# Converting float64 weights to float32 on the chip: 1024 columns at a step, on VectorE and ScalarE alone

## The chip, the cores and the metric

One core of one Trainium2 chip runs the whole program. The metric is the device time of one execution in microseconds (us). Before the change the median of three runs is 1245.48 us (1245.4 to 1246.98). The engines are TensorE (PE, its weight loads PEld), VectorE (DVE), ScalarE (ACT), GpSimd (POOL) and SyncE (SP), which issues most DMAs. Each works through its own queue in order.

## The reference

```python
xread = softmax(scale * x @ state.T) @ state            # attention, per batch and head
sread = softmax(scale * state @ x.T) @ x
x = concat([xread, sread], axis=2) -> (4352 tokens, 512)
x = (x @ w_a) * (x @ w_b) @ w_out                       # w_a, w_b: 512 x 1536, w_out: 1536 x 512
# then a top-1 mixture of 8 experts on the result:
out[mask] = gate * sigmoid * (relu(x[mask] @ w1[e]) @ w2[e])
```

The three weights `w_a`, `w_b` and `w_out` arrive as float64 (the inputs scale them with a float64 factor). TensorE has no float64, so the kernel reads them as pairs of 32-bit words (low word, high word) and builds float32 numbers from the bits.

## The kernel before, in words

Phase 1 computes attention and the first mixture matrix products for eight batches, one after the other (`main(0)` to `main(7)`), and a last part for the state rows (`main_sr`). Phase 2 is the mixture of experts. The change touches phase 1.

For one batch, `main` runs over 12 chunks f of 128 hidden columns. `s1` (line 526) makes the two products of chunk f in `ps_ab`, 12 matmuls with 512 columns. `product` turns them into one tile: ACT copies the first (`a`, line 510), DVE multiplies by the second (line 511), and `split` writes a high part on ACT (`gh`, line 261) and the rest on DVE (`gl`, line 262). `s2` (line 539) then multiplies by the rows of `w_out`, held as a high and a low part (`wo_h`, `wo_l`), again 12 matmuls. `mprep` (line 495) multiplies the states by a group of 256 columns of `w_a` and `w_b` (the tile `wab`) and `split` stores the result as `Mh` and `Ml`, which `s1` needs for the next two chunks.

The weights are converted while batch 0 is prepared and computed. `converter` is a generator: each call converts one item of 512 columns for 128 partitions. There are 36 items, 24 of `w_a` and `w_b` and 12 of `w_out`. SP loads the raw words of an item (512 KB) into one of four buffers that lie in the tiles `y` and `yT` (so `y` and `yT` in the rows can mean raw words); three items are loaded ahead. Per item:

- DVE takes the exponent from the high word (`cx`, line 180) and the mantissa (`cm`, line 183); ACT rebiases the exponent (line 186).
- The low word is added to the mantissa by one DVE instruction (line 189) or, for the items that are not in the list `dmode`, by two on ACT (lines 192, 193) and one on POOL (line 194).
- DVE puts the sign into the power of two (line 200), and POOL multiplies mantissa and power of two (line 208 into `wab`, line 204 for `w_out`). The mantissa lies 2^20 too high, and this factor is carried along and taken out later (`UNIT`).
- For `w_out`, ACT makes `wo_h` (line 219) and POOL `wo_l` (line 220).

Two lists say when items are converted. `CFG["pro"]` gives the order of the preparation of batch 0 ("c" is one item, "m" the first `mprep`, the others are parts of attention), with ten items; `CFG["conv"]` gives how many follow in each of the 24 slots of `main(0)`. From this program order a scheduler sets the order of each engine's queue, and semaphores join them.

Of the kernel before, what the change touches and what calls it, by code (L numbers as in the profile page):

```python
# [17 lines left out]
P = 128  # L18
# [6 lines left out]
DM = 512  # L25
# [4 lines left out]
NFC = DF // P  # L30
NG = DF // 256
# [2 lines left out]
ROWS = ROWW  # L34
PADID = 1 << 20
SCALE = 0.125
UNIT = 2.0**-20
BYPE = 2
CFG = {
    "dmode": [2, 4, 5, 8, 9, 12, 14, 15, 16, 17, 18, 19, 22, 23, 24, 26, 27, 28, 29, 31, 35],  # L40
    "pro": ["c", "stt", "x0", "x3", "x1", "x2", "sc", "af0", "c", "c", "c", "af1", "c", "an", "c", "ab0", "ab1", "c", "c", "m", "c", "c"],
    "conv": [1, 3, 0, 2, 3, 3, 0, 2, 0, 1, 1, 1, 0, 2, 4, 1, 0, 3, 2, 1, 4, 0, 0, 2],
    "at0": [10, 14, 10, 12, 15, 15, 15, 18, 18, 20, 21, 23, 23, 23],
    "at": [6, 7, 9, 10, 11, 13, 14, 17, 18, 15, 19, 21, 22, 23],
    "gate": [1, 2, 3, 5, 6, 7, 9, 10, 11, 17],
# [7 lines left out]
class Phase1:  # L53
# [7 lines left out]
    def consts(self):  # L61
        nc, cp = self.nc, self.cpool
        self.ident = cp.tile([P, P], F32, name="ident")
        make_identity(nc, self.ident)
        self.ones = cp.tile([P, P], F32, name="ones")
        nc.gpsimd.memset(self.ones, 1.0)
        self.tri = cp.tile([P, P], F32, name="tri")
        nc.gpsimd.affine_select(
            out=self.tri, in_=self.ones, pattern=[[1, P]], compare_op=ALU.is_gt, fill=0.0, base=0, channel_multiplier=-1
        )  # L70
        self.ramp = cp.tile([P, NE], F32, name="ramp")
        nc.gpsimd.iota(self.ramp, [[-1, NE]], base=NE, channel_multiplier=0, allow_small_or_imprecise_dtypes=True)
# [8 lines left out]
        self.rebias = cp.tile([P, 1], F32, name="rebias")  # L81
        nc.gpsimd.memset(self.rebias, -896.0 * (1 << 23))
        self.cum = cp.tile([P, NE], F32, name="cum")
        nc.gpsimd.memset(self.cum, 0.0)

    def run(self, ctx, moe2):
        tc, nc, pg = self.tc, self.nc, self.pg
        self.moe2 = moe2
        pool = lambda c, n, k=1, **kw: c.enter_context(tc.tile_pool(name=n, bufs=k, **kw))
# [13 lines left out]
        c_wo, c_wab, c_at, c_cv = (ExitStack() for _ in range(4))  # L103
# [14 lines left out]
        ab = lambda g: [(g, i, jp) for i in range(2) for jp in range(2)]  # L118
        order = ab(0) + ab(1) + [0, 1]
        for f in range(NFC):  # L120
            if f // 2 + 2 < NG:
                order += ab(f // 2 + 2)[2 * (f % 2) : 2 * (f % 2) + 2]
            if f + 2 < NFC:
                order.append(f + 2)
# [27 lines left out]

    def converter(self, order):

        nc = self.nc
        n = 512
        raws = {}

        def load(i):
            if i >= len(order):  # L160
                return
            it = order[i]
            raw = raws[i] = self.craw[i % 4]
            if isinstance(it, int):
                src = self.w_out[P * it : P * it + P, :]
                nc.sync.dma_start(out=raw, in_=src)
            else:
                g, ab, jp = it
                src = (self.w_a, self.w_b)[ab][2 * P * jp : 2 * P * jp + 2 * P, 512 * g : 512 * g + 512]
                nc.sync.dma_start(  # L170
                    out=raw.rearrange("p (a b) -> p a b", a=2), in_=src.rearrange("(j p) f -> p j f", p=P)
                )

        def first(i):
            raw = raws.pop(i)
            w = raw.rearrange("p (n two) -> p n two", two=2)
            lo, hi = w[:, :, 0].bitcast(U32), w[:, :, 1]
            ex = self.pc.tile([P, n], I32, tag="cx", name="cx")
            m = self.pc.tile([P, n], I32, tag="cm", name="cm")
            nc.vector.tensor_scalar(  # L180
                out=ex, in0=hi, scalar1=20, scalar2=0x7FF, op0=ALU.logical_shift_right, op1=ALU.bitwise_and
            )
            nc.vector.tensor_scalar(
                out=m, in0=hi, scalar1=0xFFFFF, scalar2=0x100000, op0=ALU.bitwise_and, op1=ALU.bitwise_or
            )
            nc.scalar.activation(out=ex, in_=ex, func=AF.Relu, scale=float(1 << 23), bias=self.rebias)
            mf = m.bitcast(F32)
            if i in CFG["dmode"]:
                nc.vector.scalar_tensor_tensor(out=mf, in0=lo, scalar=2.0**-32, in1=m, op0=ALU.mult, op1=ALU.add)
            else:  # L190
                tl = lo.bitcast(F32)
                nc.scalar.activation(out=tl, in_=lo, func=AF.Copy, scale=2.0**-32)
                nc.scalar.activation(out=mf, in_=m, func=AF.Copy)
                nc.gpsimd.tensor_tensor(out=mf, in0=mf, in1=tl, op=ALU.add)
            return hi, ex, mf

        def second(i, hi, ex, mf):
            it = order[i]
            exf = ex.bitcast(F32)
            nc.vector.scalar_tensor_tensor(  # L200
                out=ex, in0=hi, scalar=-(1 << 31), in1=ex, op0=ALU.bitwise_and, op1=ALU.bitwise_or
            )
            if isinstance(it, int):
                nc.gpsimd.tensor_tensor(out=mf, in0=mf, in1=exf, op=ALU.mult)
                return mf
            g, ab, jp = it
            v = lambda t: t.rearrange("p (a b) -> p a b", a=2)
            nc.gpsimd.tensor_tensor(
                out=self.wab[:, ab, 2 * jp : 2 * jp + 2, 256 * g : 256 * g + 256], in0=v(mf), in1=v(exf), op=ALU.mult
            )  # L210

        for i in range(3):
            load(i)
        for i in range(len(order)):
            load(i + 3)
            v = second(i, *first(i))
            if v is not None:
                f = order[i]
                nc.scalar.activation(out=self.wo_h[:, f, :], in_=v, func=AF.Copy)  # L219
                nc.gpsimd.tensor_tensor(  # L220
                    out=self.wo_l[:, f, :], in0=v, in1=self.wo_h[:, f, :].bitcast(F32), op=ALU.subtract
                )
            yield

    def scatter(self, **kw):
# [31 lines left out]
            nc.sync.dma_start(out=t[:, h : h + step], in_=src[:, h : h + step])  # L257
        self.at.setdefault(b, {}).update(x=t, st=st)

    def split(self, hi, lo, src, scale=1.0):  # L260
        self.nc.scalar.activation(out=hi, in_=src, func=AF.Copy, scale=scale)  # L261
        self.nc.vector.scalar_tensor_tensor(  # L262
            out=lo, in0=src, scalar=scale, in1=hi.bitcast(F32), op0=ALU.mult, op1=ALU.subtract
        )

    def aux(self, name):
        pool, tag = next(self.banks)
# [2 lines left out]
    def attention(self, b):  # L270
# [156 lines left out]
        def sread():  # L427
# [14 lines left out]
            for q in range(2):  # L442
                nc.vector.tensor_scalar(
                    out=d["sr"][:, D * q : D * q + D],
                    in0=ps[:, D * q : D * q + D],
                    scalar1=d["s2"][:, q : q + 1],
                    scalar2=UNIT,
                    op0=ALU.mult,
                    op1=ALU.mult,
                )  # L450


# [32 lines left out]
    def mprep(self, b, g):  # L485
# [14 lines left out]
                    stop=True,  # L500
                )
        for q in range(2):
            self.split(Mh[:, :, q, :], Ml[:, :, q, :], ps[q].rearrange("p (a f) -> p a f", a=2), UNIT)

    def product(self, pa, pb, n, f):
        nc, p2 = self.nc, self.p2
# [36 lines left out]
    def evac(self, b):  # L543
        nc, ys = self.nc, self.acc
        ysb = self.y
        for t, y in enumerate(ys):
            if t % 2 == 0:
                nc.scalar.activation(out=ysb[:, t, 0:DM], in_=y, func=AF.Copy, scale=UNIT)
            else:
                nc.vector.tensor_scalar(out=ysb[:, t, 0:DM], in0=y, scalar1=UNIT, scalar2=None, op0=ALU.mult)  # L550

    def slots(self, prog, n):
        it = iter(prog)
# [1256 lines left out]
```

## Time and profile before

| | |
|---|---|
| median of 3 runs | 1245.48 us |
| profiled execution | 1245.91 us, span 1244.2 us |
| PE busy in the span | 1163.8 us (94%) |
| DVE busy | 673.6 us (54%) |
| ACT busy | 442.0 us (36%) |
| POOL busy | 271.9 us (22%) |

The span is what the trace covers; the 1.7 us that the profiled execution takes beside it stay what they are. The busy shares are means over stages of different kinds. So the rows below are mostly of one stage: the time from the first `s2` matmul of batch 0 (48.6 us) to the end of batch 0 (169.2 us).

### The profile page before, as it was taken

How to read it: one execution, taken by the hardware profiler on the slowest of the kernel's cores; microseconds unless marked ns; L12 is line 12 of the kernel's file. 1: busy time of each engine (PE TensorE's matmuls, PEld its weight loads, DVE VectorE, ACT ScalarE, POOL GpSimd, SP SyncE). 2: the span in 40 equal slices, each digit the busy share in tenths (PEclk: the TensorE clock that was granted, in tenths of full speed). 3: DMA queues.
4: the chain of work that ended last, by engine and by line, in shares of the span. 5: the costliest groups of instructions: out<-in, count | busy, mean ns of one | idle time of the engine just before them, and what ended most of it. 6: DMA issues, size and time to landing. Idle time of an engine off the chain costs nothing. (4 is left out here: it accounts for less than half of the span.)

```text
span 1244.2 us, 19388 instructions
## 1 busy us (share of the span) xinstructions
PE 1163.8 (94%) x7076; PEld 911.4 (73%) x7076; DVE 673.6 (54%) x1147; ACT 442.0 (36%) x756; POOL 271.9 (22%) x346
## 2 busy tenths in 40 slices
PE   4868799999999999999999999898999999999994
PEld 2445576776776767777677789787889898888883
DVE  7999954546436455464464345653262444454553
ACT  4455542434333333333343234422141233232342
POOL 5665710100101001001010012102131312233121
PEclk7789999999999999999999999898999999999998
DMA  6354232030310302202000004565462261727600
GB/s 193 113 160 154 68 69 37 35 70 1 86 20 35 69 3 67 38 1 69 1 35 1 1 34 98 141 161 131 146 145 83 69 159 45 171 78 180 161 24 29
DMA packets 97455, 98.81 MB, mean 79 GB/s; under 512 B 58555, under 2 KB 69852, under 8 KB 97308
## 3 DMA queue, kind: packets, MB, share of 16 engines
q1 hardware_dynamic: 87508, 71.53, 22.8%
q0 software_dynamic: 9536, 25.41, 6.9%
q8 instruction: 74, 1.21, 0.4%
q14 instruction: 73, 0.60, 0.2%
q10 hardware_dynamic: 264, 0.07, 0.0%
HBM read 76.75 MB, written 21.02 MB: 79 GB/s over the span
## 5 line engine op out<-in xcount | busy, mean ns | idle before, releaser
L994 PEld LDWEIGHTS ps_h<-yT,w 128*128 128x128 f32 x1536 | 194.1, 192 | 12.4 <-issue 6.5
L994 PE MATMUL ps_h<-yT,w 128*128 128x256 f32 x1536 | 196.5, 284 | 6.2 <-issue 6.1
L1015 PE MATMUL ps_o<-w,hT 128*128 (+1 forms) x768 | 190.2, 395 | 5.2 <-DVE hT L955 5.2
L539 PE MATMUL ps_y<-wo_h,gh 128*128 128x512 f32 x408 | 168.4, 413 | 1.2 <-ACT wo_h L219 1.2
L1015 PEld LDWEIGHTS ps_o<-w,hT 128*128 128x128 f32 x768 | 139.6, 187 | 35.7 <-issue 5.8
L539 PE MATMUL ps_y<-wo_h,gl 128*128 128x512 f32 x408 | 161.3, 396 | 3.3 <-DVE gl L262 3.3
L539 PE MATMUL ps_y<-wo_l,gh 128*128 128x512 f32 x408 | 162.4, 398 | 0.0
L511 DVE TENSOR_TENSOR a<-a,ps_ab 128x512 f32<-128x512 f32 x96 | 65.5, 682 | 153.4 <-PE ps_ab L526 153.4
L526 PE MATMUL ps_ab<-Ah,Mh 128*128 128x512 f32 x384 | 130.4, 419 | 11.3 <-DVE a L511 8.5
L526 PE MATMUL ps_ab<-Al,Mh 128*128 128x512 f32 x384 | 123.6, 401 | 0.0
L526 PE MATMUL ps_ab<-Ah,Ml 128*128 128x512 f32 x384 | 123.0, 400 | 0.0
L526 PEld LDWEIGHTS ps_ab<-Ah,Mh 128*128 128x128 f32 x384 | 68.3, 193 | 64.6 <-issue 25.6
L975 POOL DMA_INDIRECT out<-yT,gt x37 | 46.6, 1258 | 306.3 <-DVE yT L965 227.8
L949 ACT ACTIVATE hT<-ps_h 128x512 fp32r<-128x512 f32 x64 | 38.0, 593 | 202.8 <-PE ps_h L994 195.1
L955 DVE SCALAR_TENSOR_TENSOR hT<-ps_h,hT 128x512 fp32r<-128x512 f32 x64 | 44.0, 687 | 110.1 <-ACT hT L949 110.1
L510 ACT ACTIVATE a<-ps_ab 128x512 f32<-128x512 f32 x96 | 57.2, 596 | 119.7 <-PE ps_ab L526 119.7
L262 DVE SCALAR_TENSOR_TENSOR gl<-a,gh 128x512 fp32r<-128x512 f32 (+1 forms) x108 | 77.6, 718 | 39.6 <-ACT gh L261 38.8
L539 PEld LDWEIGHTS ps_y<-wo_h,gh 128*128 128x128 f32 x408 | 77.5, 190 | 26.2 <-issue 7.1
L261 ACT ACTIVATE gh<-a 128x512 fp32r<-128x512 f32 (+1 forms) x108 | 65.4, 605 | 82.6 <-DVE a L511 82.5
L539 PEld LDWEIGHTS ps_y<-wo_h,gl 128*128 128x128 f32 x408 | 76.9, 189 | 22.5 <-DVE gl L262 4.1
L539 PEld LDWEIGHTS ps_y<-wo_l,gh 128*128 128x128 f32 x408 | 77.6, 190 | 17.1 <-issue 1.7
L262 DVE SCALAR_TENSOR_TENSOR Ml<-ps_m,Mh 128x512 fp32r<-128x512 f32 x96 | 61.9, 684 | 48.3 <-ACT Mh L261 48.1
(251 smaller groups left out, 1555.5 us busy)
## 6 DMA issues: line engine op xcount, KB each, us to landing
raw<-in_moe_w SPq DMA_DIRECT2D x32, 512.0 KB, 10.4
raw<-in_moe_w SPq DMA_DIRECT2D x8, 2048.0 KB, 8.8
x<-in_x SPq DMA_DIRECT2D x7, 1024.0 KB
xin<-in_x SPq DMA_DIRECT2D x96, 64.0 KB
y<-in_moe_w_a SPq DMA_DIRECT2D x8, 512.0 KB
yT<-in_moe_w_b SPq DMA_DIRECT2D x8, 512.0 KB
y<-ysort POOLq DMA_DIRECT2D x28, 128.0 KB, 6.2
y<-in_moe_w_out SPq DMA_DIRECT2D x6, 512.0 KB
```

The lines of the kernel that those rows point to most:

```text
L261: self.nc.scalar.activation(out=hi, in_=src, func=AF.Copy, scale=scale)
L262: self.nc.vector.scalar_tensor_tensor(out=lo, in0=src, scalar=scale, in1=hi.bitcast(F32), op0=ALU.mult, op1=ALU.subtract)
L510: nc.scalar.activation(out=a[:, 0:n], in_=pa[:, 0:n], func=AF.Copy)
L511: nc.vector.tensor_tensor(out=a[:, 0:n], in0=a[:, 0:n], in1=pb[:, 0:n], op=ALU.mult)
L526: nc.tensor.matmul(out=ps, lhsT=m[:, ab, q, c0 : c0 + P], rhs=r[:, q, :], start=i == 0, stop=i == 5)
L539: nc.tensor.matmul(out=y, lhsT=l[:, sl], rhs=r[:, f, :], start=f == 0 and i == 0, stop=f == NFC - 1 and i == 2)
L949: return e.activation(out=self.hT[:, j % 2, :, 0, :], in_=self.ps_h[j % 2].rearrange("p (f n) -> p f n", f=2), func=AF.Relu)
L955: return e.scalar_tensor_tensor(out=l, in0=self.ps_h[j % 2].rearrange("p (f n) -> p f n", f=2), scalar=0.0, in1=h.bitcast(F32), op0=ALU.ma ...
L975: return e.indirect_dma_start(out=self.out, out_offset=bass.IndirectOffsetOnAxis(ap=to[0:rows].bitcast(U32), axis=0), in_=self.ob[t][0:row ...
L994: m = e.matmul(out=self.ps_h[j % 2][:, G * (f % 2) : G * (f % 2) + G], lhsT=self.w1[:, wh, x : x + P], rhs=self.yT[:, c, yh, :], start=k == 0,
L1015: m = e.matmul(out=self.ps_o[2 * (k % 2) + t], lhsT=self.hT[:, j % 2, f, hh, P * t : P * t + P], rhs=self.w2c(slot, wh, 2 * j + f), start= ...
```

## The change

An item is now 1024 columns (two loads of 512 KB), and there are 18 items and two raw buffers. Per item there are five instructions. ACT scales the low word to a 16-bit integer (`cr`) and scales the high word, read as a float32, so that its exponent gets the bias of float32 (`cx`). DVE shifts `cx` left by three bits, puts the sign in (into `wab`, or `cx` for `w_out`), and adds `cr` to the lower 16 bits in place. POOL does nothing of this any more; for `w_out` the low part `wo_l` is now made by DVE. The numbers come out at their true size, so `UNIT` is gone from the later lines: `split` uses a plain subtraction, and two others become plain copies or lose a factor. The lists `pro` and `conv` are written anew: five items in the preparation, and 13 in the slots of `main(0)`.

```diff
-    "pro": ["c", "stt", "x0", "x3", "x1", "x2", "sc", "af0", "c", "c", "c", "af1", "c", "an", "c", "ab0", "ab1", "c", "c", "m", "c", "c"],
-    "conv": [1, 3, 0, 2, 3, 3, 0, 2, 0, 1, 1, 1, 0, 2, 4, 1, 0, 3, 2, 1, 4, 0, 0, 2],
+    "pro": ["c", "stt", "x0", "x3", "x1", "x2", "sc", "c", "af0", "af1", "c", "an", "c", "ab0", "ab1", "m", "c"],
+    "conv": [0, 1, 0, 1, 1, 0, 1, 1, 1, 0, 1, 1, 1, 0, 1, 1, 1, 0, 0, 1, 0, 0, 0, 0],
...
-        self.craw = [t[:, 1024 * i : 1024 * i + 1024].bitcast(I32) for t in (self.yf, self.yTf) for i in range(2)]
-        self.pc = pool(c_cv, "pc", 3)
+        self.craw = [t[:, 0:2048].bitcast(I32) for t in (self.yf, self.yTf)]
+        self.pc = pool(c_cv, "pc", 2)
...
+            r = self.pc.tile([P, n], U16, tag="cr", name="cr")
+            x = self.pc.tile([P, n], I32, tag="cx", name="cx")
+            nc.scalar.activation(out=r, in_=lo, func=AF.Copy, scale=2.0**-29)
+            nc.scalar.activation(out=x.bitcast(F32), in_=hi.bitcast(F32), func=AF.Copy, scale=2.0**-112)
+            V.tensor_scalar(out=x, in0=x, scalar1=3, scalar2=None, op0=ALU.logical_shift_left)
...
+            V.scalar_tensor_tensor(
+                out=to, in0=v(hi), scalar=-(1 << 31), in1=v(x), op0=ALU.bitwise_and, op1=ALU.bitwise_or
             )
+            V.tensor_tensor(out=half, in0=half, in1=v(r), op=ALU.add)
+            return x.bitcast(F32)
+
+        for i in range(2):
             load(i)
         for i in range(len(order)):
+            v = step(i)
+            load(i + 2)
+            if isinstance(order[i], int):
+                h, l = (t[:, 2 * order[i] : 2 * order[i] + 2, :].rearrange("p f n -> p (f n)") for t in (self.wo_h, self.wo_l))
+                nc.scalar.activation(out=h, in_=v, func=AF.Copy)
+                V.tensor_tensor(out=l, in0=v, in1=h.bitcast(F32), op=ALU.subtract)
             yield
...
-    def split(self, hi, lo, src, scale=1.0):
-        self.nc.scalar.activation(out=hi, in_=src, func=AF.Copy, scale=scale)
-        self.nc.vector.scalar_tensor_tensor(
-            out=lo, in0=src, scalar=scale, in1=hi.bitcast(F32), op0=ALU.mult, op1=ALU.subtract
-        )
+    def split(self, hi, lo, src):
+        self.nc.scalar.activation(out=hi, in_=src, func=AF.Copy)
+        self.nc.vector.tensor_tensor(out=lo, in0=src, in1=hi.bitcast(F32), op=ALU.subtract)
```

How the queues change is seen at three places. The first is DVE in batch 0, from the product of chunk 2 on (`a` and `gl` are the product's tiles, `cx` and `cm` the conversion's). Before:

```order
L511 TENSOR_TENSOR a<-a,ps_ab_477 128x512
L180 TENSOR_SCALAR cx<-yT 128x512
L183 TENSOR_SCALAR cm<-yT 128x512
L180 TENSOR_SCALAR cx<-yT 128x512
L189 SCALAR_TENSOR_TENSOR cm<-yT,cm 128x512
L262 SCALAR_TENSOR_TENSOR gl<-a,gh 128x512
L200 SCALAR_TENSOR_TENSOR cx<-yT,cx 128x512
L183 TENSOR_SCALAR cm<-yT 128x512
L200 SCALAR_TENSOR_TENSOR cx<-yT,cx 128x512
L189 SCALAR_TENSOR_TENSOR cm<-yT,cm 128x512
```

And the same place now (line numbers are those of the changed file; line 496 is the product, line 250 `split`):

```order
L496 TENSOR_TENSOR a<-a,ps_ab_384 128x512
L196 SCALAR_TENSOR_TENSOR wab<-y,cx 128x4x256
L250 TENSOR_TENSOR gl<-a,gh 128x512
L199 TENSOR_TENSOR wab<-wab,cr 128x4x256
L196 SCALAR_TENSOR_TENSOR cx<-yT,cx 128x1024
L426 RECIPROCAL s_192<-s_192 128x2
L199 TENSOR_TENSOR cx<-cx,cr 128x1024
L496 TENSOR_TENSOR a<-a,ps_ab_450 128x512
L210 TENSOR_TENSOR wo_l<-cx,wo_h 128x1024
L250 TENSOR_TENSOR gl<-a,gh 128x512
```

Between two products there stand fewer but longer instructions, and `wo_l` has come over from POOL. The second place is the head of ACT's queue, with what each row waits for. Before (DMAHW are loads, PE and DVE those engines):

```order
L192 ACT_TABLE_LOAD
L192 ACTIVATE y<-y 128x512 [waits DMAHW6_49]
L186 ACTIVATE cx<-cx,rebias 128x512 [waits DVE_49,Pool_49]
L193 ACTIVATE cm<-cm 128x512 [waits DVE_49]
L329 ACTIVATE xT<-ps_xt 128x512 [waits PE_49]
```

And now:

```order
L184 ACT_TABLE_LOAD [waits DMAHW7_49]
L184 ACTIVATE cr<-y 128x1024 [waits DMAHW6_49]
L185 ACTIVATE cx<-y 128x1024
L315 ACTIVATE xT<-ps_xt 128x512 [waits PE_49] x2
L184 ACTIVATE cr<-yT 128x1024 [waits DMAHW1_49,DMAHW0_49]
```

ACT now starts an item before DVE, not behind it, and the load of its function table stands behind the wait for the second half of the first item. The third place is PE at a `mprep` in the middle of batch 0. Before, the eight matmuls of `mprep` stand inside an `s2`:

```order
L539 MATMUL ps_y_381<-wo_h,gh 128x512
L495 MATMUL ps_m_588<-wab,stT 32x512 [waits Activation_49,Pool_49]
L495 MATMUL ps_m_589<-wab,stT 32x512 [waits Activation_49]
...
L539 MATMUL ps_y_381<-wo_l,gh 128x512
L539 MATMUL ps_y_381<-wo_h,gl 128x512
```

Now the `mprep` of the same size a little later stands directly ahead of the `s1` that needs it:

```order
L511 MATMUL ps_ab_608<-Ah,Ml 128x512 x2
L480 MATMUL ps_m_624<-wab,stT 32x512 [waits DVE_49,PE_49]
L480 MATMUL ps_m_625<-wab,stT 32x512 [waits DVE_49]
...
L511 MATMUL ps_ab_677<-Ah,Mh 128x512 [waits Activation_49]
L511 MATMUL ps_ab_684<-Ah,Mh 128x512 [waits DVE_49]
```

So `s1` there waits for ACT's `Mh` with no other matmul between. From the first row of `main(1)` on, the order on PE, ACT and SP is the same before and after.

## Rows read from the trace of the kernel before

**Rows 1.** The page: busy tenths in 40 slices of the span.

```profile
PE   4868799999999999999999999898999999999994
DVE  7999954546436455464464345653262444454553
```

**Rows 2.** Stretches: from:to and length, busy us (instructions) by engine, granted clock, DMA.

```profile
48.60:169.20 120.60, 92.97 (x508) 61.46 (x506) 113.53 (x156) 61.16 (x108) 74.65 (x50) 0.92 0.39 113
252.90:334.30 81.40, 81.40 (x508) 59.12 (x507) 42.35 (x80) 29.06 (x53) 7.41 (x14) 1.00 0.16 41
```

**Rows 3.** Groups by line, 48.6 to 169.2, DVE: busy us, mean ns, idle before.

```profile
L262 DVE SCALAR_TENSOR_TENSOR gl<-a,gh 128x512 fp32r<-128x512 f32 x12 | 14.5, 1205 | 0.4 <-ACT gh L261 0.4
L200 DVE SCALAR_TENSOR_TENSOR cx<-yT,cx 128x512 int32<-128x512 int32 x14 | 13.0, 930 | 0.2 <-ACT cx L186 0.2
L180 DVE TENSOR_SCALAR cx<-yT 128x512 int32<-128x512 int32 x13 | 9.4, 722 | 0.2 <-DMA yT<-in_moe_w_out 0.2
L189 DVE SCALAR_TENSOR_TENSOR cm<-y,cm 128x512 f32<-128x512 uint32 x6 | 5.2, 865 | 0.0
```

**Rows 4.** Timeline of DVE: start us, length us, instruction.

```profile
71.72 0.41 DVE L180 TENSOR_SCALAR cx<-y 128x512 int32<-128x512 int32 x1
72.05 1.51 DVE L183 TENSOR_SCALAR cm<-y 128x512 int32<-128x512 int32 x1
...
73.83 0.68 DVE L189 SCALAR_TENSOR_TENSOR cm<-y,cm 128x512 f32<-128x512 uint32 x1
74.43 1.77 DVE L200 SCALAR_TENSOR_TENSOR cx<-y,cx 128x512 int32<-128x512 int32 x1
```

**Rows 5.** Groups by line, 48.6 to 169.2, PE.

```profile
L539 PE MATMUL ps_y<-wo_h,gh 128*128 128x512 f32 x48 | 20.5, 428 | 1.2 <-ACT wo_h L219 1.2
L495 PE MATMUL ps_m<-wab,stT 64*32 64x512 f32 x80 | 11.8, 722 | 5.7 <-DVE xT L331 2.0 <-DVE Al L262 1.8 <-POOL wab L208 1.4
L466 PE MATMUL ps_srt<-ident,sr 128*128 128x128 f32 x1 | 0.3, 270 | 0.0
```

**Rows 6.** Timeline of PE: start us, length us, instruction, [idle before].

```profile
33.95 2.16 PE L526 MATMUL ps_ab<-Ah,Mh 128*128 128x512 f32 x3 [0.21 <-ACT Ah L261]
...
48.56 0.39 PE L539 MATMUL ps_y<-wo_h,gh 128*128 128x512 f32 x1
...
53.21 0.62 PE L526 MATMUL ps_ab<-Ah,Mh 128*128 128x512 f32 x2
...
58.78 0.62 PE L526 MATMUL ps_ab<-Ah,Mh 128*128 128x512 f32 x2
...
75.20 0.99 PE L526 MATMUL ps_ab<-Ah,Mh 128*128 128x512 f32 x2 [1.37 <-ACT Mh L261]
...
81.26 1.22 PE L526 MATMUL ps_ab<-Ah,Mh 128*128 128x512 f32 x2 [4.62 <-DVE a L511]
...
136.41 0.94 PE L360 MATMUL ps_af<-ident,sc 128*128 128x128 f32 x6 [3.12 <-DVE sc L351]
```

**Rows 7.** Groups by line, 0 to 250: instructions of 1024 columns and line 186.

```profile
L186 ACT ACTIVATE cx<-cx,rebias 128x512 int32<-128x512 int32 x36 | 25.6, 716 | 31.3 <-DVE cx L180 31.2
L262 DVE SCALAR_TENSOR_TENSOR Al<-AT,Ah 128x1024 fp32r<-128x1024 f32 x1 | 1.2, 1226 | 0.6 <-ACT Ah L261 0.6
L261 ACT ACTIVATE Ah<-AT 128x1024 fp32r<-128x1024 f32 x1 | 1.1, 1060 | 2.3 <-DVE AT L384 2.3
```

**Rows 8.** A load of 512 KB alone: its issue on SP, then DMA's share and GB/s.

```profile
52.98 0.37 SPq L170 DMA_DIRECT2D yT<-in_moe_w_b  x1
```

**Rows 9.** Stretches of 1 us: clock, DMA share, GB/s.

```profile
55.00:56.00 1.00, 1.00 0.99 381
56.00:57.00 1.00, 1.00 0.14 53
```

**Rows 10.** Timeline, start of the program: DVE's second raw half, ACT's table load.

```profile
2.77 1.28 ACT L192 ACT_TABLE_LOAD   x1 [2.77 <-issue]
...
10.13 0.43 DVE L180 TENSOR_SCALAR cx<-y 128x512 int32<-128x512 int32 x1 [0.55 <-DMA y<-in_moe_w_a]
```

More of the change, by code (lines that the diff above doesn't have):

```diff
@@ L12 @@
 U32 = mybir.dt.uint32
+U16 = mybir.dt.uint16
 AF = mybir.ActivationFunctionType
@@ L80, in consts @@
             )
-        self.rebias = cp.tile([P, 1], F32, name="rebias")
-        nc.gpsimd.memset(self.rebias, -896.0 * (1 << 23))
         self.cum = cp.tile([P, NE], F32, name="cum")
@@ L117, in run @@
             )
[L118 to L124, printed above, removed]
+        order = []
+        for g in range(NG):
+            order += [(g, 0), (g, 1)] + [g - 1] * (g > 0)
+        order.append(NG - 1)
         self.conv = self.converter(order)
@@ L155, in converter @@
         nc = self.nc
-        n = 512
+        V = nc.vector
+        n = 1024
         raws = {}
@@ L162, in load @@
             it = order[i]
[L163 to L171, printed above, removed]
-                )
@@ L174, in first @@
-        def first(i):
+            raw = raws[i] = self.craw[i % 2]
+            for k in range(2):
+                to = raw[:, n * k : n * k + n]
+                if isinstance(it, int):
+                    f = 2 * it + k
+                    nc.sync.dma_start(out=to, in_=self.w_out[P * f : P * f + P, :])
+                else:
+                    g, ab = it
+                    src = (self.w_a, self.w_b)[ab][2 * P * k : 2 * P * k + 2 * P, 512 * g : 512 * g + 512]
+                    nc.sync.dma_start(
+                        out=to.rearrange("p (a b) -> p a b", a=2), in_=src.rearrange("(j p) f -> p j f", p=P)
+                    )
@@ L175, in first, with step @@
+        def step(i):
             raw = raws.pop(i)
+            it = order[i]
             w = raw.rearrange("p (n two) -> p n two", two=2)
             lo, hi = w[:, :, 0].bitcast(U32), w[:, :, 1]
[L178 to L181, printed above, removed]
-            )
-            nc.vector.tensor_scalar(
-                out=m, in0=hi, scalar1=0xFFFFF, scalar2=0x100000, op0=ALU.bitwise_and, op1=ALU.bitwise_or
-            )
@@ L186, in first @@
[L186 to L210, printed above, removed]
@@ L212, in converter @@
-        for i in range(3):
+            r = self.pc.tile([P, n], U16, tag="cr", name="cr")
[3 more added lines that the diff above has]
+            V.tensor_scalar(out=x, in0=x, scalar1=3, scalar2=None, op0=ALU.logical_shift_left)
+            if isinstance(it, int):
+                to, v = x, lambda t: t
+                half = x.bitcast(U16).rearrange("p (n two) -> p n two", two=2)[:, :, 0]
+            else:
+                g, ab = it
+                v = lambda t: t.rearrange("p (j f) -> p j f", j=4)
+                to = self.wab[:, ab, :, 256 * g : 256 * g + 256].bitcast(I32)
+                half = self.wab.bitcast(U16)[:, ab, :, 512 * g : 512 * g + 512]
+                half = half.rearrange("p j (f two) -> p j f two", two=2)[:, :, :, 0]
@@ L213, in converter @@
+            V.scalar_tensor_tensor(
+                out=to, in0=v(hi), scalar=-(1 << 31), in1=v(x), op0=ALU.bitwise_and, op1=ALU.bitwise_or
+            )
+            V.tensor_tensor(out=half, in0=half, in1=v(r), op=ALU.add)
+            return x.bitcast(F32)
+        for i in range(2):
             load(i)
         for i in range(len(order)):
[L215 to L222, printed above, removed]
+            v = step(i)
[4 more added lines that the diff above has]
+                V.tensor_tensor(out=l, in0=v, in1=h.bitcast(F32), op=ALU.subtract)
@@ L446, in sread @@
                     scalar1=d["s2"][:, q : q + 1],
-                    scalar2=UNIT,
+                    scalar2=None,
                     op0=ALU.mult,
-                    op1=ALU.mult,
                 )
@@ L502, in mprep @@
         for q in range(2):
-            self.split(Mh[:, :, q, :], Ml[:, :, q, :], ps[q].rearrange("p (a f) -> p a f", a=2), UNIT)
+            self.split(Mh[:, :, q, :], Ml[:, :, q, :], ps[q].rearrange("p (a f) -> p a f", a=2))
     def product(self, pa, pb, n, f):
@@ L547, in evac @@
             if t % 2 == 0:
-                nc.scalar.activation(out=ysb[:, t, 0:DM], in_=y, func=AF.Copy, scale=UNIT)
+                nc.scalar.activation(out=ysb[:, t, 0:DM], in_=y, func=AF.Copy)
             else:
-                nc.vector.tensor_scalar(out=ysb[:, t, 0:DM], in0=y, scalar1=UNIT, scalar2=None, op0=ALU.mult)
+                nc.vector.tensor_copy(out=ysb[:, t, 0:DM], in_=y)
     def slots(self, prog, n):
```

3 lines of the change are left out of this document (removed).

## The prediction

> **What bounds the kernel now.** I read the busy slices first. PE stands at 9 from the sixth slice on; only ahead of that, to about 155 us, is it lower, and there DVE is high [rows 1]. A change in the conversion can only move that part. The stretches give its size: from the first `s2` of batch 0 at 48.56 us [rows 6] to 169.2 the program needs 120.60 us, in which DVE is busy 113.53 and PE 92.97 at a mean clock of 0.92. A later batch takes 81.40, with PE busy all of it and DVE 42.35 [rows 2]. So batch 0 is bound by DVE, and all later batches by PE. PE's timeline shows it: 4.62 us idle at 81.26 until DVE's product is there [rows 6].
>
> Why DVE is full is seen in its groups. The eight groups of lines 180, 183, 189 and 200 add to 78.6 us in the stretch; the largest and the smallest stand in [rows 3]. Their instructions come in two lengths: 0.41 or 1.51 us for the one-source ones, 0.68 or 1.77 for the two-source ones [rows 4]; the long ones lie beside POOL's tensor instructions, and POOL is busy 74.65 us [rows 2]. At the short lengths 26 items would cost 26 x (0.41 + 0.41 + 0.68) + 16 x 0.68 = 49.9 us; so about 28.7 us of the 78.6 is DVE held up beside POOL. The subtraction for `gl` suffers too, 1205 ns instead of 0.68 [rows 3, 4], 12 times, 6.3 us.
>
> **The change part by part: DVE.** Removed: the 78.6 us, and with POOL gone from the conversion the 6.3 us. The rest of DVE is 113.5 - 78.6 - 6.3 = 28.6 us. Added: 13 items of 1024 columns, each a shift, a sign merge and an add, and six `wo_l`. The shift is one-source: twice 0.41 is 0.82 at most, 0.68 if the fixed part is paid once. A two-source instruction of 1024 columns took 1226 ns [rows 7]; I take this for the sign merge and `wo_l`. The add on 16-bit numbers is not in the trace. Its lower bound is 0.68, the one-source estimate; its upper bound 1.77, the longest row of a merge [rows 4]. I take 1.23, the row of the same number of columns and two sources. Sum: 13 x (0.82 + 1.23 + 1.23) + 6 x 1.23 = 50.0, with the rest 78.6 us; with the add at 0.68 it is 71.5, at 1.77 it is 85.6.
>
> The Trainium skill ("VectorE: DVE Perf Modes", "What auto-detection actually checks") says that a two-source instruction runs at two elements per cycle only if every tensor is 16-bit with step 1. Here one input and the output take every second 16-bit number, so by the rule the add has full length; at its two-element rate the add would cost, by an estimate from that page, about 0.6 us, and DVE's sum would be some 8 us lower. No row shows a 16-bit operand; the full length is the value taken above.
>
> **ACT.** Added in the stretch: 13 x 2 instructions of 1060 ns [rows 7] and six for `wo_h`, 33.9 us. Removed, among others, 26 of line 186 at 716 ns [rows 7], 18.6 us. Even if nothing else went, ACT would be at 61.16 - 18.6 + 33.9 = 76.5 us [rows 2]. If integer forms of 1024 columns cost twice 716 ns, 1.43 us each, 26 x 0.37 = 9.6 us come on top: 86.1, as much as PE below. But lines 192, 193 and 219 go as well, so ACT is not the bound.
>
> **PE: what is late next.** One `s1` and one `s2` at full clock are 58.78 - 53.21 = 5.57 us for 24 matmuls [rows 6], 0.232 each. The stretch holds ten `s1` and twelve `s2`: 264 x 0.232 = 61.3 us. The other nine groups of PE there, from `mprep` with 11.8 us to the smallest with 0.3 [rows 5], add 23.7 us. PE's floor is 85.0 us. It is above DVE's 78.6, so PE becomes the bound, and 120.6 - 85.0 = 35.6 us is the most that the stretch can give back.
>
> It will not all come. DVE at 78.6 of 85 has little slack, and both run in order. I price three kinds of wait that the new order keeps or makes. Three `mprep` now stand directly ahead of the `s1` that needs them; such a wait was 1.37 us at 75.20 [rows 6], so 4.1. The attention of batch 1 has a chain over scores, copy and transposes, 3.12 us at 136.41 [rows 6]; I keep it whole. About 1 us is for the lower clock behind such a gap. Coupling: 8 us, between 1 (all hidden) and 20 (DVE late at half of the twelve chunks, some 3 us each).
>
> Forecast for the stretch: 85 + 8 = 93 us, 27.6 less.
>
> **Loads.** A load of 512 KB issued at 52.98 flows at 381 GB/s and is over in the slice from 56 [rows 8, 9], about 3.4 us. The second half of an item adds 512 KB at 381 GB/s, 1.4: 4.8 us. A raw buffer is held for load, two ACT instructions, shift and merge: 4.8 + 2.1 + 0.8 + 1.2 = 8.9 us. Two buffers then give an item every 4.5 us, 13 in 58 us, under PE's 85. In the stretch before, DVE waited 0.2 us for a load [rows 3].
>
> **The preparation.** Here work gets less but the chain longer. The second raw half lands at 10.13; ACT's table load of 1.28 us was done at 4 [rows 10] and now stands behind it: 11.4. ACT's two instructions: 13.5; DVE's step of item 0, 3.3: 16.8. Then DVE has in its order, until `Ah` can be made, three more steps (9.9) and the softmax: eight instructions of about 0.68, one maximum over 1024 columns of 1.2, two short ones, 7.4 in all: 34.1. PE's transposes and ACT's two copies give about 2 more: the first `s1` at 36, against 33.95 [rows 6]. Before, that `s1` then stood still for its `Ml`; now this is there by then, and the two `s1` and `mprep` ahead of the first `s2` run through: at half clock 24 x 0.46 = 11.1, and 2: 49 against 48.56. I take no difference, with bounds of -4 and +4.
>
> **The rest.** The plain subtractions and copies in place of those with a factor are two-source or read PSUM as before; they lie in batches in which PE never waits [rows 2]. Nothing is gained, and nothing can be lost while DVE is at 42 of 81 us. From batch 1 on the queues of PE, ACT and SP are the same, so the gain is kept to the end.
>
> **Sum.** 1245.9 (the profiled execution, 0.4 over the median) - 27.6 = 1218.3; against the median, 1218 us. Its own range, with coupling 1 to 16 and preparation -4 to +4: 1208 to 1228.
>
> **Rivals.** (1) DVE stays the bound. If the adds cost 1.77 and the shift is also slower, DVE needs 86 to 91 us; before, it was busy for 94% of its stretch [rows 2], and with PE's chains beside it 85 to 90% is likelier: 97 to 107 us, so 1222 to 1232, and up to 1236 where the preparation loses 4 more. For: DVE's sum is only 6 us below PE's floor. Against: these prices are each above the nearest row.
> (2) PE's floor is reached: a stretch of 86 us and a preparation 2 us shorter: 1209. For: later batches run without a gap. Against: there DVE is half empty.
> (3) Slower: the two large buffers bind. Before, four small buffers let three loads run ahead; now a load starts only when the merge two steps back is done, and every one of ACT's and DVE's instructions on the raw words stands in a queue behind products. With w us of queueing per buffer, 13 items need 6.5 x (8.9 + w). From w = 9.7 on this is more than the 120.6 of before; at w = 11 it is 129 us, 1255. For: ACT's reading of the raw words stands ahead of other work in its queue and holds it up while a load is under way. Against: a slot of `main(0)` is about 2.8 us of matmuls, so a queue of 9.7 us is more than three slots of work, on every item.
>
> **How the numbers follow.** The forecast has 0.65, rival (1) 0.18, rival (2) 0.10, rival (3) 0.04; 0.03 is left for a time near that of before, where (1) and (3) meet. Range for 8 in 10: from rival (2) to the middle of rival (1), 1208 to 1232. A measurement of this kernel tells apart about 0.2%, 2.5 us. Faster: 0.65 + 0.18 + 0.10 = 0.93; same 0.03; slower 0.04.
>
> **What would show it.** Right: batch 0 ends near 142 us; DVE is busy some 78 us between the first `s2` and that end; no row of a 512-column one-source or two-source DVE instruction near 1.5 us in it; PE's clock there near 1.00; the first `s2` between 44 and 53; later batches at 81.4. Wrong: PE idle until DVE in many chunks (rival 1, seen in the length of the add), or ACT and DVE idle until raw words land (rival 3). The forecast falls if the add or ACT's integer instructions are far from the rows of 1024 columns.

## The result, and the profile after

The changed kernel takes 1206.12 us (median of 4 runs, 1205.36 to 1208.24) against 1245.52 us (4 runs, 1245.4 to 1246.98): a ratio of 0.9684, interval 0.9667 to 0.9701. The forecast was 1218 us with a range of 1208 to 1232. The direction and the place of the gain were right; the time lies 12 us below the forecast and 2 us below the lower end of the range.

The profiled execution took 1205.72 us with a span of 1204.1. Its slices answer to [rows 1]:

```profile
PE   3898999999999999999999999789999999999994
DVE  5889545465464364554643354842443444454462
```

PE now reaches 9 in the third slice, not in the sixth. The stretches, in the columns of [rows 2]: the preparation up to the first `s2`, the rest of batch 0, a later batch.

```profile
0.00:45.73 45.73, 23.30 (x122) 14.22 (x122) 29.43 (x38) 22.70 (x30) 8.57 (x26) 0.70 0.58 189
45.73:133.30 87.57, 78.79 (x514) 57.55 (x507) 77.95 (x104) 56.33 (x79) 2.41 (x2) 0.98 0.48 151
217.10:298.50 81.40, 81.40 (x507) 59.14 (x507) 42.28 (x79) 29.06 (x53) 7.41 (x14) 1.00 0.17 41
```

The rest of batch 0 fell from 120.6 to 87.6 us. DVE's busy time there fell from 113.53 to 77.95 and POOL's from 74.65 to 2.41; a later batch takes 81.40 us as before [rows 2]. The spans differ by 40.1 us, and this is where they lie (the changes are taken before rounding):

| | before | after | change | forecast |
|---|---|---|---|---|
| start to the first `s2` | 48.56 | 45.73 | -2.8 | 0 |
| first `s2` to the end of batch 0 | 120.6 | 87.6 | -33.1 | -27.6 |
| end of batch 0 to the end of phase 1 | 622.1 | 622.8 | +0.7 | 0 |
| phase 2 | 452.9 | 448.0 | -4.9 | 0 |

The groups of DVE in batch 0, which answer to [rows 3, 7]:

```profile
L199 DVE TENSOR_TENSOR wab<-wab,cr 128x1024 uint16<-128x1024 uint16 x8 | 11.0, 1370 | 0.1
L186 DVE TENSOR_SCALAR cx<-cx 128x1024 int32<-128x1024 int32 x12 | 8.3, 690 | 2.7 <-ACT cx L185 2.5
L250 DVE TENSOR_TENSOR gl<-a,gh 128x512 fp32r<-128x512 f32 x12 | 8.2, 682 | 1.4 <-ACT gh L249 1.4
L210 DVE TENSOR_TENSOR wo_l<-cx,wo_h 128x1024 fp32r<-128x1024 f32 x6 | 7.3, 1222 | 0.9 <-ACT wo_h L209 0.9
L196 DVE SCALAR_TENSOR_TENSOR wab<-yT,cx 128x1024 int32<-128x1024 int32 x3 | 3.7, 1225 | 0.0
```

The second length of [rows 4] is gone from these groups: `gl` is at 682 ns, where it was 1205 [rows 3]. A long row is left in one place, where POOL and DVE each multiply one half of `A` (POOL from 110.1 us, DVE from 110.9; ns shortest/median/longest):

```profile
L382 POOL TENSOR_TENSOR A<-A,sm x1: 1812/1812/1812, 110.1 to 110.1; 128x512 f32<-128x512 f32 x1
L382 DVE TENSOR_TENSOR A<-A,sm x1: 1545/1545/1545, 110.9 to 110.9; 128x512 f32<-128x512 f32 x1
```

### The profile page after: what moved, and what is told of

Read it like the earlier page. It is cut to its first block, busy times and chain, and to the rows that moved or that the text cites. A ratio compares the mean times of both kernels' runs of the same rounds, so it can differ in the third digit from the quotient of the medians.

```text
span 1204.1 us, 19174 instructions
## 1 busy us (share of the span) xinstructions
PE 1141.3 (95%) x7076; PEld 906.3 (75%) x7076; DVE 628.6 (52%) x1078; ACT 437.9 (36%) x720; POOL 178.3 (15%) x282
## 5 line engine op out<-in xcount | busy, mean ns | idle before, releaser
L979 PEld LDWEIGHTS ps_h<-yT,w 128*128 128x128 f32 x1536 | 191.4, 191 | 12.2 <-issue 6.4
L979 PE MATMUL ps_h<-yT,w 128*128 128x256 f32 x1536 | 193.6, 283 | 6.1 <-issue 6.0
L524 PE MATMUL ps_y<-wo_h,gh 128*128 128x512 f32 x408 | 165.9, 411 | 2.0 <-ACT wo_h L209 2.0
L250 DVE TENSOR_TENSOR gl<-a,gh 128x512 fp32r<-128x512 f32 (+1 forms) x108 | 71.3, 660 | 41.0 <-ACT gh L249 40.3
L250 DVE TENSOR_TENSOR Ml<-ps_m,Mh 128x512 fp32r<-128x512 f32 x96 | 61.8, 686 | 48.3 <-ACT Mh L249 48.2
```

Source lines behind the costliest of these rows:

```text
L250: self.nc.vector.tensor_tensor(out=lo, in0=src, in1=hi.bitcast(F32), op=ALU.subtract)
L524: nc.tensor.matmul(out=y, lhsT=l[:, sl], rhs=r[:, f, :], start=f == 0 and i == 0, stop=f == NFC - 1 and i == 2)
L979: m = e.matmul(out=self.ps_h[j % 2][:, G * (f % 2) : G * (f % 2) + G], lhsT=self.w1[:, wh, x : x + P], rhs=self.yT[:, c, yh, :], start=k == 0,
```

## The experiments

All were made with the same four numbers in view: the first `s2`, the end of batch 0 (VectorE's second copy of `ps_y`), the end of phase 1, and the total. A run that repeats the changed kernel shows how far they move by themselves:

> The changed kernel once more, as it is, to see how its stages vary from one execution to another. Phase 2 was 4.8 us shorter in its profile than in that of the kernel before, though its code is the same. If this is chance of one execution (transfers landing a little earlier or later), the length of phase 2 here lies anywhere between the two, 446 to 452 us; if it belongs to the kernel, within 1 us of 446.5.

Measured: 1206.57 us (1206.32 to 1210.46), ratio 0.9692 (0.9669 to 0.9715). First `s2` at 44.99 (45.73 in the first profile), end of batch 0 at 132.4 (133.3), end of phase 1 at 755.1 (756.1). So a shift of about 1 us in these marks is nothing. Phase 2 took 449.6 us, between the first profiles of the two kernels, as the forecast for chance has it; more on this at the end of the section.

**Does POOL's work cost VectorE its time?** Multiplications of 128x512 whose result nobody reads are put on POOL behind the items of batch 0; the queues of PE, DVE, ACT and SP stay as they are.

```diff
...
+            for _ in range(3 if i >= 5 and i not in (14, 15) else 0):
+                nc.gpsimd.tensor_tensor(out=o, in0=src, in1=o, op=ALU.mult)
```

> The changed kernel, with 33 extra GpSimd multiplies of 128x512 beside it in batch 0: three behind each of 11 items, into a tile that nobody reads; the queues of TensorE, VectorE and ScalarE are the same row for row. Theory H (the gain is that VectorE is no longer held up by GpSimd): before, 48 GpSimd tensor instructions in the stretch went with some 35 us of longer VectorE rows, 0.73 us each, so VectorE's busy time in the stretch from the first s2 to the end of batch 0 grows from 78 by about 24 to 102 us, the short lengths get long partners again, TensorE waits for VectorE, and the program takes 1221 to 1229 us. Rival C (the gain is the shorter chain over fewer engines, and GpSimd's presence costs nothing): 1205 to 1208 us and VectorE still near 78 us.

> As the run with 33 extra GpSimd multiplies, with 11. Theory H: VectorE's busy time in the stretch grows by about 8 us to 86, of which half is absorbed since TensorE is the bound there: 1208 to 1213 us. Rival C: 1205 to 1208 us.

Measured: 1224.36 us with 33 of them, ratio 0.983 (0.9805 to 0.9856), and 1211.91 with 11 (one per item), ratio 0.9716 (0.9691 to 0.974); both as theory H had it. The stretch of batch 0 with 33:

```profile
44.59:148.70 104.11, 84.58 (x515) 60.23 (x508) 98.76 (x104) 56.99 (x79) 64.88 (x35) 0.92 0.40 128
```

DVE runs the same 104 instructions as after the change, in the same order, and they take 98.76 us in place of 77.95: 20.8 us from 33 POOL instructions, 0.63 each. With 11 it is 83.85, 0.54 each. Which instructions suffer is seen in `split` and in the product (per operation: ns shortest/median/longest, first and last start):

```profile
L259 DVE TENSOR_TENSOR gl<-a,gh x12: 665/1382/1780, 44.6 to 143.7; 128x512 fp32r<-128x512 f32 x12
L259 DVE TENSOR_TENSOR Ml<-ps_m,Mh x12: 672/680/705, 45.8 to 141.2; 128x512 fp32r<-128x512 f32 x12
L505 DVE TENSOR_TENSOR a<-a,ps_ab x11: 669/675/707, 45.2 to 142.3; 128x512 f32<-128x512 f32 x11
```

`gl` and `Ml` are the same operation of the same size on the same line. `gl` has both inputs in SBUF and has up to 1780 ns; `Ml` and the product read one input from PSUM, and none of them has more than 707, though POOL runs beside most of them. The shift has one input, in SBUF, and lengthened too: 985 ns on average, where it was 690 after the change.

```profile
L188 DVE TENSOR_SCALAR cx<-cx 128x1024 int32<-128x1024 int32 x12 | 11.8, 985 | 0.0
```

So the second length in [rows 4] does come from POOL's work, and the forecast's term for it stands; 33 POOL instructions bring back 18 of the 39 us. The Trainium skill ("SBUF — State Buffer", "Who interferes with whom") says that a VectorE instruction with two SBUF inputs contends with a GpSimd instruction that reads SBUF, and one with at most one SBUF input outside the two-port modes does not; the rows of `gl`, `Ml` and the product agree, 665 to 1780 ns against 672 to 707.

**The same from the other side.** In the kernel before, POOL's additions, multiplications and `wo_l` are given to VectorE, in the old method with its 512 columns:

```diff
-    "dmode": [2, 4, 5, 8, 9, 12, 14, 15, 16, 17, 18, 19, 22, 23, 24, 26, 27, 28, 29, 31, 35],
+    "dmode": list(range(36)),
...
-                nc.gpsimd.tensor_tensor(out=mf, in0=mf, in1=exf, op=ALU.mult)
+                nc.vector.tensor_tensor(out=mf, in0=mf, in1=exf, op=ALU.mult)
...
```

> The kernel before, with its whole conversion but no GpSimd tensor instruction in it: the adds, the multiplies and the low part of w_out go to VectorE. Theory H: VectorE runs at its short lengths, 26 items at 2.86 us and 11 low parts at 0.68, 82 us, with the rest 110 us, against 113.5 with GpSimd's help, so the program takes 1235 to 1250 us, though VectorE does half as much again. Rival P (GpSimd's help was worth its holds): VectorE has 32 us more to do in the stretch, 1265 to 1285 us.

Measured: 1237.11 us (1235.41 to 1237.73), ratio 0.992 (0.9897 to 0.9942). DVE has 202 instructions in the stretch in place of 156 and yet is busy 105.16 us, not 113.53. POOL's help took more of VectorE than it gave. This is 9 of the 39 us. The rest came with the new method as a whole: without POOL in both, VectorE is busy 105.16 us there and 77.95 with the new one.

**The width of 1024 columns, and the factors.** The changed kernel at 512 columns (36 items, four raw buffers), and with the factor 1.0 written back into `split` and two other lines:

```diff
-        n = 1024
+        n = 512
...
```

> The changed kernel at 512 columns an item: 36 items, four raw buffers, two items wherever there was one. Theory H: VectorE needs some 6 us more in the stretch (the fixed part of each instruction twice), 84 us, TensorE is still the bound: 1204 to 1212 us; the preparation may gain 1 to 2 us since the first 512 columns land earlier. Rival G (the gain comes from fewer, larger instructions): at least half of it is lost, above 1225 us.

```diff
-        self.nc.vector.tensor_tensor(out=lo, in0=src, in1=hi.bitcast(F32), op=ALU.subtract)
+        self.nc.vector.scalar_tensor_tensor(
+            out=lo, in0=src, scalar=1.0, in1=hi.bitcast(F32), op0=ALU.mult, op1=ALU.subtract
+        )
...
```

> The changed kernel with the forms of before put back where the factor was taken out: split and the other lines multiply by 1.0. The theory that these edits weigh nothing expects no difference from the changed kernel, 1204 to 1208 us, and split's instructions of 512 columns at 0.68 to 0.69 us as now. A rival (the plain forms are cheaper on VectorE where TensorE waits for it) expects 2 to 5 us more.

Measured: 1205.98 us, ratio 0.967 (0.9642 to 0.9697), and 1206.26, ratio 0.9684 (0.966 to 0.9707). Neither changes the time. At 512 columns the first `s2` came at 40.24, 5 us earlier, but batch 0 ended at 132.5 all the same.

**Where do PE's last 9 us of idle time come from?** PE is busy 78.79 of 87.57 us. Its longest waits after the change (us in total, times, longest):

```profile
PE ps_ab L511 <- ACT Mh L249: 6.0, 4, 2.2
PE ps_y L524 <- ACT wo_h L209: 2.0, 2, 1.8
```

The first theory was the order on PE: the three `mprep` that stand directly ahead of their `s1`. One number moves all `mprep` ahead; and a second edit has the table of ACT loaded before the first raw words.

```diff
-    "mp0": 3,
+    "mp0": 4,
```

> The changed kernel with each mprep of batch 0 one slot earlier. If the waits of s1 for Mh (6.0 us in four places) are there because mprep stands directly ahead of it, they shrink to about 1 us and the program takes 1200 to 1203 us. Rival: mprep then waits for the conversion of its group instead, and the time is 1205 to 1210 us.

```diff
+        warm = self.cpool.tile([P, 1], F32, name="warm")
+        nc.gpsimd.memset(warm, 0.0)
+        nc.scalar.activation(out=warm, in_=warm, func=AF.Copy)
```

> The changed kernel with a ScalarE instruction on one column at the very start, so that the function table is loaded while the first weights are under way. If the preparation is one chain from the first item on, the first s2 comes about 1.3 us earlier and the program takes 1204 to 1205.5 us; if the chain has slack there (a later load sets the end), no difference.

The theory missed in both. With `mp0` 4 the total is 1208.46 us, ratio 0.9699 (0.9677 to 0.972), and batch 0 ends at 132.6. The waits for `Mh` shrank, and others came, behind `mprep` itself:

```profile
PE ps_m L480 <- DVE sm L378: 2.5, 1, 2.5
PE ps_ab L511 <- ACT Mh L249: 2.3, 2, 1.5
PE ps_m L480 <- DVE wab L199: 0.9, 1, 0.9
```

With the early table 1209.16 us, ratio 0.9707 (0.9685 to 0.9728): ACT's first item starts 1.4 us earlier (10.30 against 11.71 in the repeat), the first `s1` 0.7 (35.80, 36.48), the first `s2` 0.1 (44.89, 44.99), and batch 0 ends at 132.3. So the time won at the head of the queue was lost again before the end of batch 0.

So VectorE was the suspect: from 20 to 125 us it is busy 97.9 of 105 in the repeat. Three edits take work from it. The first has ScalarE prepare the sign and joins the shift to the merge.

```diff
-            V.tensor_scalar(out=x, in0=x, scalar1=3, scalar2=None, op0=ALU.logical_shift_left)
+            nc.scalar.activation(out=hi.bitcast(F32), in_=hi.bitcast(F32), func=AF.Copy, scale=0.0)
...
-                out=to, in0=v(hi), scalar=-(1 << 31), in1=v(x), op0=ALU.bitwise_and, op1=ALU.bitwise_or
+                out=to, in0=v(x), scalar=3, in1=v(hi), op0=ALU.logical_shift_left, op1=ALU.bitwise_or
```

> The shift is joined to the sign merge: ACT makes a signed zero of the high word in place (scale 0.0), and one VectorE instruction does shift and OR, so VectorE loses 13 x 0.69 = 9.0 us in the stretch of batch 0 and ScalarE gains 13 x 1.12 = 14.6. Theory D (after the change VectorE is still what is late: it has hardly any idle time from 60 to 127 us, and PE's waits for Mh and wo_h are only where its lateness shows): the stretch goes from 87.5 to 80 to 83 us, the first phase ends at 748 to 752 instead of 755 to 756, total 1199 to 1203. Rival Q (PE's order and the chain through ScalarE make these waits): no gain, and up to 5 us of loss from the longer ScalarE queue, total 1206 to 1212.

```diff
+            w = n if i < 5 else 8
-            V.tensor_scalar(out=x, in0=x, scalar1=3, scalar2=None, op0=ALU.logical_shift_left)
+            V.tensor_scalar(out=x[:, :w], in0=x[:, :w], scalar1=3, scalar2=None, op0=ALU.logical_shift_left)
```

> The shift is cut to 8 columns in the 13 items converted during batch 0, so those weights are not shifted; ScalarE has the same work as in the changed kernel. VectorE loses about 13 x 0.6 = 8 us. Only the first phase can be compared, since the values that choose the experts differ. Theory D: the first phase ends at 747 to 751 us (755 to 756 in the changed kernel). Rival Q: 754 to 757.

```diff
-            nc.scalar.activation(out=r, in_=lo, func=AF.Copy, scale=2.0**-29)
+            nc.scalar.activation(out=lo, in_=lo, func=AF.Copy, scale=7.49 * 2.0**-32)
...
-            V.tensor_scalar(out=x, in0=x, scalar1=3, scalar2=None, op0=ALU.logical_shift_left)
+            V.scalar_tensor_tensor(
+                out=x, in0=x, scalar=3, in1=lo.bitcast(I32), op0=ALU.logical_shift_left, op1=ALU.bitwise_or
+            )
...
-            V.tensor_tensor(out=half, in0=half, in1=v(r), op=ALU.add)
```

> Three VectorE instructions per item become two: ScalarE leaves three bits of the low word (0 to 7, scale 7.49 x 2^-32) in place, one VectorE instruction shifts the high word and ORs these bits in, the second puts in the sign; the 16-bit add goes. By the rows of the changed kernel an item costs VectorE 2 x 1.22 in place of 0.69 + 1.22 + 1.37, 0.84 us less, 10.9 us over 13 items; ScalarE's work is the same. Theory D (VectorE is what is late in the stretch): the first phase ends at 748 to 751.5 us, a little below the run with the short shift (751.7), total 1199 to 1203. Rival Q (PE's order and ScalarE's chain): the first phase ends at 754 to 757, total 1205 to 1208. If the OR on words of step two costs 1.5 us or more, the gain is under 5 us of VectorE and the end lies between the two.

The first makes weights of other values than meant, so only its first phase is compared: its end is at 763.9 us, 8 to 9 later than after the change. VectorE's sum fell (70.94 us in the stretch), but ScalarE's rose to 69.45, and PE waits 8.7 us for `Mh`, which stands in ScalarE's longer queue. More than half of the delay lies ahead of the stretch: the first `s2` came at 50.41, 5.4 us later than in the repeat. Theory D missed. The second, which leaves weights unshifted and is compared in its first phase too, ends phase 1 at 751.7, some 4 us earlier, and of the waits for `Mh` 0.7 us are left. This is just above what theory D gave, and spoke for VectorE. It doesn't single VectorE out, though: with the shorter shift a raw buffer is free earlier too, and the scheduler gave PE another order in this run. The third took still more from VectorE (68.58 us in the stretch) and ends batch 0 at 132.4 again, in 1206.59 us, ratio 0.9678 (0.9654 to 0.9702), as rival Q had it. Here VectorE waits, from 20 to 125 us:

```profile
DVE cx L185 <- ACT cx L184: 10.4, 8, 3.9
DVE a L496 <- PE ps_ab L511: 7.9, 5, 4.8
```

and ScalarE, in the stretch, for raw words in the second large buffer:

```profile
ACT yT L183 <- DMA yT<-in_moe_w_out: 4.1, 2, 2.7
...
ACT yT L183 <- DMA yT<-in_moe_w_b: 4.0, 2, 2.9
```

So two limits seemed to stand one behind the other. The next runs ease both: two instructions per item and 512 columns, with four, five and six raw buffers of half the size. Of the edit, the lines of the fifth buffer:

```diff
...
+        xr = pool(c_cv, "xr")
+        self.craw += [xr.tile([P, 1024], I32, name=f"raw{i}") for i in range(1)]
...
```

> The two-instruction conversion again, at 512 columns per item, 36 items and four raw buffers of half the size: the base for the next two. Theory B (after the change the raw buffers set the pace: a buffer is held from the issue of its load to the sign merge, about 12 us for two buffers, so an item comes every 6 us whatever VectorE's sum is): the first phase ends at 753 to 756 us, as in all runs so far that keep this hold time, total 1203 to 1208. Rival Q (the order on PE): the same here.

> The same with a fifth raw buffer of 4 KB per partition, so that loads run one half item further ahead. Theory B: items come up to a fifth faster; ScalarE's waits for raw words, 8 us in the run at 1024 columns, fall to under 4, and the first phase ends 2 to 5 us earlier than with four buffers, at 749 to 752. Rival Q: it ends within 1 us of the run with four buffers, and what ScalarE no longer waits for loads it waits for something else.

> Six raw buffers, for which one of the four buffers of cx goes. Theory B: at least as early an end of the first phase as with five, 747 to 752 us. Rival Q: 754 to 757 us; later than with four buffers if the missing cx buffer binds.

Measured: 1195.15, 1195.9 and 1194.99 us; ratios 0.9604 (0.957 to 0.9638), 0.96 (0.9571 to 0.9629) and 0.9611 (0.9574 to 0.9647). These three beat both kernels. The low three bits are scaled by 7.49/8 in them, and in the run before them, so that a weight can be one unit of its last place lower. All three forecasts of theory B missed, and those of rival Q too: with four buffers batch 0 already ended 10 us earlier, and a fifth and a sixth change it by under 2 us, with no order among them.

| | columns, raw buffers | DVE in the stretch | batch 0 ends | phase 1 ends |
|---|---|---|---|---|
| three VectorE instructions per item, repeat | 1024, 2 | 78.20 | 132.4 | 755.1 |
| three | 512, 4 | 80.75 | 132.5 | 754.9 |
| two | 1024, 2 | 68.58 | 132.4 | 754.8 |
| two | 512, 4 | 71.55 | 122.3 | 744.8 |
| two | 512, 5 | 70.87 | 120.5 | 743.0 |
| two | 512, 6 | 70.57 | 121.9 | 744.3 |

With two instructions at 512 columns PE's longest wait in the stretch is 1.8 us, and it is busy 78.85 of 83.59 us:

```profile
38.71:122.30 83.59, 78.85 (x514) 57.73 (x507) 71.55 (x121) 59.87 (x110) 1.47 (x2) 0.98 0.52 161
```

Shown is that either edit alone gives nothing and both together 10 us. That the large buffers are the limit in the run with two instructions at 1024 columns is not shown. For it speak ScalarE's waits for raw words in the stretch, 12.0 us in all there and 4.8 with small buffers; but with three instructions and small buffers they are 9.8. A third large buffer was not tried, and with such edits the scheduler lays the queues out anew.

**Phase 2.** Its instructions are the same in all kernels, yet the first two profiles differ by 4.9 us there.

> The kernel before, unchanged, profiled again. The second phase (from the end of phase 1 to the end of the span) took 452.9 us in the first profile of it and 448.0 in that of the changed kernel, with the same instructions. If that difference is the spread from run to run, it now takes anything from 447 to 454 us; if it belongs to the kernels, 452 to 454. First phase 789 to 792 us in either case.

Measured: 455.3 us (from 792.2 to 1247.5), above both forecasts. Three profiles with the old method have 452.9, 455.3 and 453.6; twelve with the new one 447.5 to 453.5, with a mean of 449.7, and one of them within the range of the three. The repeat of before and the first profile of the changed kernel, in the columns of [rows 2]:

```profile
792.20:1247.50 455.30, 420.87 (x2564) 373.76 (x2564) 207.07 (x333) 133.46 (x194) 108.76 (x138) 0.96 0.43 110
```

```profile
756.10:1204.10 448.00, 416.55 (x2564) 370.64 (x2564) 206.93 (x332) 133.49 (x194) 108.68 (x138) 0.97 0.44 112
```

So part of the 4.9 us is spread, and the means of the two methods lie some 4 us apart. PE's busy time differs by 4.3 us for the same 2564 matmuls; DVE's, ACT's and POOL's hardly differ. One part can be pinned down. Counted from the end of the program, the same 600 matmuls in the middle of phase 2, all at a granted clock of 1.00, follow each other in 94.60 us in each of the three profiles of the old method (from 961.89 us in the first) and 94.19 in eleven of the twelve of the new one (from 923.63). The twelfth is the run with the early table: it has the new method and 94.60. Over phase 2 this makes some 1.8 us, an estimate from these figures. It goes with the program and not with the single execution, but not with the method as such. What sets it, and where the rest lies, stays open.

## Why the prediction was too high

**Which step held.** The forecast's reading of batch 0 was right in the main: the gain is VectorE's time, much of it time beside POOL, and PE's work then fills 90% of the stretch. DVE's sum was put at 78.6 us and is 77.95. The terms in it were off in both ways: the shift 0.69 in place of 0.82, the 16-bit add 1.35 to 1.37 in place of 1.23, the merge and `wo_l` 1.22 as said. The coupling, 8 us, is 87.57 - 78.79 = 8.8. That the sum came so near is luck in part: of what it was made of, only the waits for `Mh` were as named (6.0 us for 4.1); the 3.1 us of the attention chain are gone, and `wo_h` with 2.0 was not named.

**Which step failed first: PE's floor, "the other nine groups add 23.7 us".** It took the busy time of `mprep` from [rows 5] as work, 11.8 us. A row of `mprep` before, with its weight loads on PEld (start, length; idle before in brackets), shows what is in that number:

```profile
98.17 1.73 PE L495 MATMUL ps_m<-wab,stT 64*32 64x512 f32 x9
99.24 0.18 PEld L495 LDWEIGHTS ps_m<-wab,stT 64*32 64x32 f32 x14 [0.93 <-DVE srT L467]
```

(The view ends within the first row; the whole row is 2.15 us with 16 matmuls.) Two matmuls were issued, then PE stood 0.93 us, and the row counts it as busy, since a row joins instructions that follow each other and their ends are modelled. PE after the change, where nothing holds it there:

```profile
36.85 1.22 PE L511 MATMUL ps_ab<-Ah,Mh 128*128 128x512 f32 x2
...
41.29 0.79 PE L511 MATMUL ps_ab<-Ah,Ml 128*128 128x512 f32 x2
41.91 0.61 PE L511 MATMUL ps_ab<-Ah,Mh 128*128 128x512 f32 x2
42.36 0.62 PE L511 MATMUL ps_ab<-Al,Mh 128*128 128x512 f32 x2
...
57.89 1.09 PE L480 MATMUL ps_m<-wab,stT 64*32 64x512 f32 x16
```

The 16 matmuls take 1.09 us, and the group in the stretch 6.1 us, not 11.8:

```profile
L480 PE MATMUL ps_m<-wab,stT 64*32 64x512 f32 x87 | 6.1, 600 | 0.0
```

The row above is one of seven that make up the 11.8 us. Four of them hold such a gap, of 0.46 to 0.93 us. Two of the five `mprep` are split in two, and a part of eight or even two matmuls takes 1.04 to 1.06 us as well. In one row, of 2.70 us, the granted clock was 0.50, the level of 1.2 GHz. So the number held waits, splits and a lower clock beside the work. With these 5.7 us less the floor is 79.3 (with all nine groups as they are after the change, 16.9 us, it is 78.2), and PE's busy time is 78.79. That is the miss in batch 0: 93 forecast, 87.57 measured, the coupling being 0.8 us larger.

**The preparation, "no difference".** The first `s1` was put at 36 and came at 36.85. But the two `s1` behind it were priced at half clock, 11.1 us. Rows of two matmuls begin 0.86 us apart up to 41 us and 0.45 from 41.91 on. The granted clock was 0.50, the level of 1.2 GHz, from 36.85 to 41.3 us, in which PE worked without a gap, and 1.00, that of 2.4 GHz, from 41.91 on. They took 44.72 - 36.85 = 7.9 us, and the first `s2` came 2.8 us earlier than before. The bound of -4 held it.

**Phase 2, "the gain is kept to the end".** It was kept, and 4.9 us more came in the profile; the forecast had no term for that, and the runs explain it only in part. The floor or this was enough, each by itself, to take the time below the range: 4.9 us more would have given some 1211 us, and 5.7 more some 1212. The ends of the range are not quite the sum of its bounds either: 1245.9 - (120.6 - 86) - 4 is 1207.3 and 1218.3 + 8 + 4 is 1230.3, where the forecast says 1208 and 1228.

**The rivals.** That VectorE stays the bound was given 0.18 by the price of its instructions. The prices were near, and still VectorE is 93% busy from 20 to 125 us. Of the three runs that relieve it, one ends batch 0 earlier (129.3 us for 132.4), and two don't. The forecast counted it only from the first `s2` on; that it is full from 20 us, in the preparation, and carries along what it owes then, is a reading that no run tests. The buffers as a limit, the rival on the slower side, seem to exist too: smaller ones alone (512 columns) gave nothing in the changed kernel, and 10 us once VectorE had two instructions per item. The floor rival, 1209 us, came nearest in time, and that is luck: there, too, the floor was 85, with a coupling of 1 us where 8.8 was measured.

## What to carry to other kernels

Before a busy time becomes a floor, compare its group's time per instruction with a stretch in which nothing is waited for, and look at the weight loads between. When a POOL instruction reads SBUF, charge VectorE's instructions beside it, those with two inputs in SBUF above all: here 0.5 to 0.6 us for each POOL instruction, which made POOL's share of the work a loss. When fewer instructions alone give nothing and smaller items alone give nothing, try both at once; here each alone gave 0 and both gave 10 us.

## What the runs showed of the hardware that was not expected

- A 16-bit add of two inputs of 1024 numbers at step two took 1.35 to 1.37 us; two-input instructions of 1024 32-bit numbers took 1.22. It was not shorter, but 0.13 to 0.15 longer.
- A bitwise OR of a shifted word with every second 32-bit word costs the same as any two-input instruction: 1.22 us for 1024 numbers, 0.68 for 512.
- ScalarE's conversion of 1024 32-bit integers took 1.13 to 1.14 us on average, as much as its float instruction on words of step two (1.14); twice the 716 ns of [rows 7] had been the upper bound.
- VectorE's subtraction took 672 to 705 ns with one input in PSUM and 665 to 1780 with both in SBUF, beside the same POOL work.
- The same 600 matmuls of phase 2, at a granted clock of 1.00 in all runs, took 94.60 us in four profiles and 94.19 in eleven. The value goes with the program.
